# The last step of a running sum taken into the TensorE product that reads it, and a division moved behind the second layer

## The chip, the cores and the metric

The kernel runs on one core of one Trainium2 chip. The metric is the device time of one execution in microseconds (us), median of several runs. The engines of the core are named as in the profile: PE (TensorE, matrix products into PSUM), DVE (VectorE), ACT (ScalarE), POOL (GpSimd) and SP, which here only issues transfers. Transfers run on the core's 16 DMA engines.

## The reference

Two stages. First an attention read between tokens `x` (8 batches, 8 heads, 512 tokens, 64 wide) and a state of 32 rows: each token reads the state (`xread`) and each state row reads the tokens (`sread`). Both results together, 4352 rows of 512, are the input of a mixture of experts with soft slots:

```python
logits = x @ phi                          # 4352 x 32 slots
d = exp(logits - logits.max(0)); d /= d.sum(0) + 1e-9
slot_input = (d.T @ x).reshape(E, 4, D)   # 8 experts, 4 slots each
for e in range(E):
    h = np.maximum(slot_input[e] @ w1[e], 0.0)   # w1: 8 x 512 x 1024
    slot_out[e] = h @ w2[e]                      # w2: 8 x 1024 x 512
c = softmax(logits, axis=1)
out = c @ slot_out
```

All data is fp32. The weights w1 and w2 are 16.8 MB each, `x` is 8.4 MB, and the output is 4352 rows of 2 KB.

## The kernel before

The attention stage goes batch by batch. Its steps are short functions, and the string `ORDER` writes down in which order they are issued (`T.3` is step `T` of group 3). Every engine runs its own instructions in that order. Batches go in pairs, four groups in all; each group gives a part of the logits and, without a second pass over the tokens, a part of `slot_input`.

The sum over tokens runs as a streaming softmax. `nm_all` holds the running maximum, `al_all` the factor by which the old sums shrink when the maximum grows, `l_row` the running sum of exponentials and `y` the running sum of weighted inputs, kept in 128 partitions as (4 parts of 32 slots) x 128. A group's step is: `T` (PE) makes `t_ps`, the attention weights multiplied into the exponentials; `tt` (DVE) turns its 32 x 32 blocks out of PSUM; `Px` (PE) multiplies by the state into `px_ps`; `Y` (DVE) does `y = y * al + px_ps`. The state rows add two steps of their own (`Ps`, `Ys`).

After the last group, `Wd` multiplies `l_row` by a matrix of ones and zeros (`rep`) into `l_ps` to add the 4 parts, `We` (DVE, two instructions, L633 and L634) adds 1e-9 and takes the reciprocal `rl`, `Yf` (ACT, L638) makes a diagonal matrix `rd` of `rl`, and `SI` (PE, L642) is one product of `y` and `rd`: it transposes `y` and divides by l together. `SIe` copies the four blocks of its result to `si_m` by four DVE copies. `si_m` is the stationary operand of the first layer (L697, `h_ps`). The steps `W.256` and `W.128` are products of the identity whose results nobody reads.

Then both layers run for all experts with the weights as moving operand: the first layer in two halves (`h_ps`), a turn and the ReLU, the second layer (`so_ps`, L760), and `so_sum`, which adds 4 row blocks by `rep` (`sum_ps`) and copies the result to `so_r` by ACT (L788). From `so_r` and the softmax `c` come the output tiles (`o`), copied by ACT and DVE and sent by SP (L809, L811, L834, L852).

Buffers: the small PSUM results share one tag `ms` with three buffers, taken in turn (`mtile`). A new tile waits until all readers of the tile three before it are done. The weights stream from HBM the whole time through SP into the pools `big` and `pairs`; a weight transfer is issued when its buffer is free. The pool `const` lies ahead of them in SBUF; each of its tiles is rounded up to 32 bytes a partition, and with its sizes as they are the pool `big` starts at a multiple of 512 bytes.

Of the kernel before, what the change touches and what calls it, by code (L numbers as in the profile page):

```python
# [8 lines left out]
F32 = mybir.dt.float32  # L9
# [6 lines left out]
P = 128  # L16
B = 8
S = 512
NS = 32
D = 64  # L20
# [30 lines left out]
mul.7.1 R.6.0 x1.6.0 R.6.1 mk.2 bm.2 U.1 l1.6.0 ae.5.1 nme.2 mul.7.0 rr.6 srT.7 ae.4.0 sr.6 mul.6.0 dx.2 A.4.1 aT.7.0  # L51
srT.6 aT.6.0 srTe.7 dT.2 srTe.6 Px.1 dTe.2 mul.6.1 Ls.1 V.1 Lse.1 Ue.1 Y.1 Lr.1 ae.4.1 Lx.6.0 aT.6.1 al.2 Lx.6.1
Lx.7.0 T.2 aT.7.1 msx.1 Lx.7.1 Ve.1 tt.2 dsx.1 A.6.1 pv.3 Lu.1 als.1 mx.3 mkd.3 ae.6.1 A.7.1 bm.3 nme.3 keep.3 Lu.2
Lus.1 A.7.0 lkp.1 A.6.0 dx.3 D.1 dT.3 ad.7.1 Px.2 ad.6.0 ae.7.0 dTe.3 Ps.1 al.3 Y.2 Ys.1 Lu.3 T.3 tt.3 Wd We Px.3
W.256 Yf Y.3 SI W.128 SIe
"""
SR_BUFS = 1
AN = 2
# [5 lines left out]
def attention_soft_moe(ctx: ExitStack, tc: tile.TileContext, x0, x1, x, st0, st1, w1, w2a, w2b, out_x, out_s):  # L64
# [7 lines left out]
    pe, act, dve, pool = nc.tensor, nc.scalar, nc.vector, nc.gpsimd  # L72

    cp = ctx.enter_context(tc.tile_pool(name="const", bufs=1))
# [9 lines left out]
    for b in range(B):  # L84
        t = big.tile([P, 4, NJ, 2 * D], F32, tag="big", name=f"x{b}")
        if b == 0:
            for i in range(4):
                v = x0[i].rearrange("p (g j c) -> p g j c", g=1, j=NJ)
# [58 lines left out]
    ident = cp.tile([P, P], F32, name="ident")  # L147
# [16 lines left out]
    G_sb = cp.tile([P, B, 2, NS], F32, name="G_sb")  # L164
# [5 lines left out]
    al_all = cp.tile([P, B + 2], F32, name="al_all")  # L170
    l_row = cp.tile([P, 1], F32, name="l_row")
    y = cp.tile([P, P], F32, name="y")

    with ExitStack() as actx:
        wk = actx.enter_context(tc.tile_pool(name="work", bufs=1))
        sm = actx.enter_context(tc.tile_pool(name="small", bufs=2))
# [4 lines left out]
        Q = [dict() for _ in range(2)]  # L181
        X2 = [dict(b=g) for g in GROUPS]
# [5 lines left out]
        Z = {"n": 0}  # L188

        def half(name):  # L190
            return wk.tile([P, S], F32, tag="h", name=name, bufs=NH)

        def mtile(shape, name):
            return ps_m.tile(shape, F32, tag="ms", name=name)
# [119 lines left out]
        def copy_of(eng):  # L314
            return act.copy if eng is act else dve.tensor_copy
# [313 lines left out]
            pe.matmul(Z["lp"], rep, l_row, start=True, stop=True)  # L629

        def We():
            Z["rl"] = sm.tile([P, 1], F32, tag="rl", name="rl", bufs=1)
            dve.tensor_scalar_add(Z["rl"], Z["lp"], EPS)  # L633
            dve.reciprocal(Z["rl"], Z["rl"])  # L634

        def Yf():
            Z["rd"] = sm.tile([P, P], F32, tag="ds", name="rd", bufs=1)
            act.mul(Z["rd"], ident, Z["rl"])  # L638

        def SI():  # L640
            Z["p"] = mtile([P, 4, NS], "si_ps")
            pe.matmul(Z["p"].rearrange("p k n -> p (k n)"), y, Z["rd"], start=True, stop=True)  # L642

        def warm(n):
            p = ps_t.tile([P, S], F32, tag="tr", name=f"warm{n}_ps")
# [4 lines left out]
        def slots(t, k):  # L650
            lead = 32 if k else 0
            v = t[:, 256 * k - lead : 256 * k - lead + 288]
            return v.rearrange("p (e c) -> p e c", c=36)[:, :, lead : lead + 4]

        si_m = []

        def windows():
            for k in range(2):
                si_m.append(half(f"si_m{k}"))
                pool.memset(si_m[k], 0.0)  # L660

        def SIe():
            for k in range(4):
                dve.tensor_copy(slots(si_m[k // 2], k % 2), Z["p"][:, k, :].rearrange("p (e c) -> p e c", c=4))

        steps = dict(
            G=G, Ge=Ge, X=X, xe=xe, S=Sc, q=q, m1=m1, sub=sub, x1=x1, l1=l1, rr=rr, mul=mul, aT=aT, m2=m2, e2=e2,
            E=E_, ee=ee, A=A_, ae=ae, R=R_, sr=sr, srT=srT, srTe=srTe, Lx=Lx, keep=keep, mx=mx, mk=mk,
            pv=pv, bm=bm, nme=nme, al=al, dx=dx, Lu=Lu, dT=dT, dTe=dTe, T=T_, tt=tt, U=U, Ue=Ue, Px=Px, Y=Y,
            Ls=Ls, Lse=Lse, Lr=Lr, msx=msx, als=als, dsx=dsx, Lus=Lus, lkp=lkp, D=Dn, V=V, Ve=Ve, Ps=Ps, Ys=Ys,  # L670
            xd=xd, ed=ed, ad=ad, srTd=srTd, Wd=Wd, We=We, Yf=Yf, SI=SI, SIe=SIe, windows=windows, mkd=mkd, W=warm, keepd=keepd, dTd=dTd, Ud=Ud, Vd=Vd,
        )
        load_w(NBIG - B + 2 * NPAIR)
        order = ORDER.split()
# [55 lines left out]
        c = [half(f"c{i}") for i in range(3)]  # L730
        c = [v[:, 0 : t.shape[1]].rearrange("p (t n) -> p t n", n=NS) for v, t in zip(c, c_t)]
# [22 lines left out]
        so, so_sb, so_r = {}, {}, {}  # L754
# [26 lines left out]
        def so_sum(k, half_of=0):  # L781
            c = slice(P * half_of, P * half_of + P)
            p = mtile([P, P], f"sum_ps{k}_{half_of}")
            pe.matmul(p, rep, so_sb[k][:, c], start=True, stop=True)
            i = k + half_of
            if i % 2 == 0:
                so_r[i // 2] = half(f"so_r{i // 2}")[:, 0:256]
            act.copy(so_r[i // 2][:, P * (i % 2) : P * (i % 2) + P], p)  # L788

        def out(k, q):  # L790
            hf, col = k // 2, 128 * (k % 2)
# [96 lines left out]
        so_copy(0)  # L888
        more(1)
        so_sum(0)  # L890
        more(1)
        so_sum(0, 1)
        out(0, 0)
        more(5)
# [4 lines left out]
        so_copy(2)  # L899
        out(1, 1)  # L900
        so_sum(2)
        more(4)
        out_st(0)
# [46 lines left out]
```

## Time and profile before

| | |
|---|---|
| median of 3 runs | 129.68 us (129.62 to 129.85) |
| the profiled execution: its time, and its span from first to last instruction | 129.54 us, 127.8 us |
| busy share of the span: PE, DVE, ACT, POOL | 91%, 68%, 60%, 35% |
| bytes moved, mean rate over the span | 51.74 MB, 405 GB/s |
| granted clock of PE | 1.00 until 121 us, then 0.50; mean 0.974 |

The span is what the trace's times count in; 1.74 us of the execution lie around it. Times in the rows below are us from the span's start.

### The profile page before, as it was taken

What the parts mean: (1) busy time and instruction counts of PE and PEld (TensorE: products, weight loads), DVE (VectorE), ACT (ScalarE), POOL (GpSimd) and SP (SyncE); (2) the same over time, 40 slices, a digit from 0 to 9 for tenths busy, and PEclk for the clock granted to TensorE, in tenths of its full rate; (3) what the DMA queues carried; (4) which work ended last, traced back from release to release, by engine and by line L of the source; (5) the groups of instructions that cost most, each with busy time, mean ns of one, the idle gap of its engine ahead of it and who ended that gap; (6) DMA issues with size and microseconds to landing.
All of it is one profiled execution on the core that took longest, in us unless ns stands there. A gap on an engine that the chain in (4) does not pass through costs nothing.

```text
span 127.8 us, 4698 instructions
## 1 busy us (share of the span) xinstructions
PE 116.7 (91%) x1992; PEld 80.5 (63%) x1992; DVE 86.7 (68%) x194; ACT 76.9 (60%) x189; POOL 44.8 (35%) x63
## 2 busy tenths in 40 slices
PE   5989999999999999999999999999999999998600
PEld 2737686789686869858767869952465655575200
DVE  2348999999999999999986759019930355442700
ACT  4039999999999999999965711310100445635700
POOL 3005266391947467557882105803500000000000
PEclk9999999999999999999999999999999999999955
DMA  4999999999999999999999999999999999999993
GB/s 130 345 410 423 423 426 423 428 423 421 423 423 426 416 436 416 421 431 418 426 418 433 416 421 398 448 423 441 413 441 415 436 383 412 421 419 420 386 430 139
DMA packets 8229, 51.74 MB, mean 405 GB/s; under 512 B 912, under 2 KB 1040, under 8 KB 3216
## 3 DMA queue, kind: packets, MB, share of 16 engines
q1 hardware_dynamic: 7920, 50.92, 95.9%
q10 hardware_dynamic: 288, 0.52, 1.1%
q8 instruction: 15, 0.25, 0.7%
q14 instruction: 6, 0.05, 0.1%
HBM read 42.53 MB, written 8.91 MB: 403 GB/s over the span
## 4 chain that ended last, share of the span: by engine, by line
PE 72%; DVE 10%; DMA 6%; ACT 3%; issue 2%; SPq 1%; POOL 0%; DVEq 0%; ACTq 0%; POOLq 0%
PE so_ps L760 12%; PE h_ps L697 11%; PE xt_ps L226 8%; PE o L796 7%; DMA st_phi<-st_in 6%; PE sc L245 5%; PE sr_ps L343 4%; PE an_ps L309 4%; PE eT_ps L309 4%; PE lt L378 3%; PE t_ps L503 2%; DVE sums L274 2%; DVE q L258 2%; DVE aT L290 1%; DVE m L263 1%
## 5 line engine op out<-in xcount | busy, mean ns | idle before, releaser
L267 POOL TENSOR_TENSOR q<-q,m 128x512 f32<-128x512 f32 x16 | 16.8, 1051 | 15.7 <-DVE m L263 5.2
L231 ACT ACTIVATE xt<-xt_ps 128x512 f32<-128x512 f32 x30 | 18.0, 618 | 5.7 <-PE xt_ps L226 5.5
L226 PE MATMUL xt_ps<-ident,x 128*128 128x128 f32 x128 | 18.4, 282 | 0.5 <-DMA x<-x_in 0.5
L285 POOL TENSOR_TENSOR q<-q,rr 128x512 f32<-128x512 f32 x16 | 16.6, 1051 | 5.1 <-DVE rr L280 3.6
L226 PEld LDWEIGHTS xt_ps<-ident,x 128*128 128x128 f32 x128 | 14.6, 144 | 3.8 <-PE sc L245 1.4
L760 PE MATMUL so_ps<-w,h_m 128*32 128x128 f32 (+1 forms) x376 | 15.5, 309 | 0.0
L807 DVE COPY out<-o 128x512 f32<-128x512 f32 x14 | 9.2, 687 | 9.0 <-PE o L796 8.8
L760 PEld LDWEIGHTS so_ps<-w,h_m 128*32 128x32 f32 x376 | 10.4, 110 | 7.2 <-issue 4.6
L697 PE MATMUL h_ps<-w,si_m 128*32 128x512 f32 x128 | 14.4, 594 | 0.1
L296 DVE TENSOR_REDUCE nm<-sc 128x1 f32<-128x512 f32 x16 | 10.6, 670 | 2.2 <-PE sc L245 2.2
L806 ACT COPY out<-o 128x512 f32<-128x512 f32 x14 | 7.7, 588 | 6.8 <-PE o L796 6.7
L697 PEld LDWEIGHTS h_ps<-w,si_m 128*32 128x32 f32 x128 | 9.1, 110 | 3.9 <-issue 2.9
L301 ACT ACTIVATE e<-sc,nm 128x512 f32<-128x512 f32 x16 | 11.3, 709 | 0.4 <-DVE nm L296 0.2
L258 DVE STREAM_TRANSPOSE q<-sc 128x512 f32<-128x512 f32 x16 | 11.1, 695 | 0.1
L290 DVE STREAM_TRANSPOSE aT<-q 128x512 f32<-128x512 f32 x16 | 10.9, 689 | 0.3 <-POOL q L285 0.2
L343 PE MATMUL sr_ps<-x,eT 128*32 128x64 f32 x512 | 10.5, 221 | 0.1
L274 DVE TENSOR_REDUCE sums<-q 128x16 f32<-128x512 f32 x16 | 10.4, 663 | 0.2 <-ACT q L270 0.2
L263 DVE TENSOR_REDUCE m<-q 128x16 f32<-128x512 f32 x16 | 10.4, 658 | 0.0
L270 ACT ACTIVATE q<-q 128x512 f32<-128x512 f32 x16 | 10.4, 650 | 0.0
L309 PE MATMUL eT_ps<-ident,e 128*128 128x128 f32 x64 | 9.8, 279 | 0.0
L245 PE MATMUL sc<-xt,st_phi 64*32 64x512 f32 x128 | 9.6, 601 | 0.0
L343 PEld LDWEIGHTS sr_ps<-x,eT 128*32 128x32 f32 x512 | 8.7, 110 | 1.5 <-issue 1.0
(126 smaller groups left out, 186.2 us busy)
## 6 DMA issues: line engine op xcount, KB each, us to landing
w<-w_in SPq DMA_DIRECT2D x16, 1024.0 KB, 19.7
w<-w2b_in SPq DMA_DIRECT2D x4, 2048.0 KB, 15.0
x<-x_in SPq DMA_DIRECT2D x7, 1024.0 KB, 13.9
w<-w2a_in SPq DMA_DIRECT2D x6, 1024.0 KB, 19.5
out_x<-out SPq DMA_DIRECT2D x6, 1024.0 KB, 5.8
out_x<-out SPq DMA_DIRECT2D x4, 512.0 KB, 4.7
w<-w2a_in SPq DMA_DIRECT2D x4, 256.0 KB, 14.5
x<-x_in ACTq DMA_DIRECT2D x2, 256.0 KB, 3.9
```

The source lines that it names most:

```text
L226: pe.transpose(p[:, P * j : P * j + P], xb[b][:, g, j, :], ident)
L231: act.mul(r[f"xt{g}"], r[f"xp{g}"], 0.125)
L245: pe.matmul(r[f"sp{h}"][32 * g : 32 * g + 32, :], st_t(b, g)[64 * h : 64 * h + 64, :], r[f"xt{g}"][64 * h : 64 * h + 64, :], start=True, s ...
L258: dve.transpose(r[f"q{h}"], r[f"sp{h}"])
L267: pool.tensor_tensor(v, v, R[b][f"m1{h}"].broadcast_to([P, 16, NS]), op=ALU.subtract)
L274: dve.tensor_reduce(out=v, in_=R[b][f"qv{h}"], axis=AX.X, op=ALU.add)
L285: pool.tensor_tensor(v, v, r.broadcast_to([P, 16, NS]), op=ALU.mult)
L290: dve.transpose(r[f"aT{h}"], r[f"q{h}"])
L309: pe.transpose(p[:, j, :], r[f"{src}{h}"][:, P * j : P * j + P], ident)
L343: pe.matmul(r["srp"][32 * g : 32 * g + 32, h, :], r[f"eT{h}"][:, j, 32 * g : 32 * g + 32], xb[b][:, g, j, D * h : D * h + D], start=(j == ...
L697: pe.matmul(h_ps[hf][32 * kt : 32 * kt + 32, :], si_m[kt // 2][:, 256 * (kt % 2) + 32 * e : 256 * (kt % 2) + 32 * e + 32], w1t[hf, e, kt], ...
L760: pe.matmul(so[k][32 * i : 32 * i + 32, :], h_m[hf][:, 256 * i + 32 * e : 256 * i + 32 * e + 32], w(i), start=(hf == 0 and e == 0), stop=( ...
```

## The change

The last group's step of `y` is no longer done by DVE. `Yf` now makes a diagonal of the last group's factor `al` in place of `rl`. `SIa` multiplies `y` by it (4 products into two PSUM tiles, left open), and `SIb` adds to the same tiles the state times the last group's turned `t_ps` (4 products). For that `ttz` writes the turned blocks into a zeroed tile `tz`, the upper 64 partitions to one place and the lower 64 to another (two DVE transposes). `tz` reuses half of `G_sb`, zeroed on POOL in the step `windows`. `Px.3`, `Y.3`, `tt.3` and the two `W` steps are gone. `Wd` and `We` stand between `SIa` and `SIb`; `rl` is now used in `so_sum`, where ACT multiplies by it in place of copying, and it lives in the pool `const`. Two of the four copies of `SIe` move to ACT.

```diff
-Lus.1 A.7.0 lkp.1 A.6.0 dx.3 D.1 dT.3 ad.7.1 Px.2 ad.6.0 ae.7.0 dTe.3 Ps.1 al.3 Y.2 Ys.1 Lu.3 T.3 tt.3 Wd We Px.3
-W.256 Yf Y.3 SI W.128 SIe
+Lus.1 A.7.0 lkp.1 A.6.0 dx.3 D.1 dT.3 ad.7.1 Px.2 ad.6.0 ae.7.0 dTe.3 Ps.1 al.3 Y.2 Yf Ys.1 Lu.3 T.3 ttz SIa Wd We SIb
+SIe
...
         def We():
-            Z["rl"] = sm.tile([P, 1], F32, tag="rl", name="rl", bufs=1)
+            Z["rl"] = cp.tile([P, 1], F32, name="rl")
...
         def Yf():
             Z["rd"] = sm.tile([P, P], F32, tag="ds", name="rd", bufs=1)
-            act.mul(Z["rd"], ident, Z["rl"])
-
-        def SI():
-            Z["p"] = mtile([P, 4, NS], "si_ps")
-            pe.matmul(Z["p"].rearrange("p k n -> p (k n)"), y, Z["rd"], start=True, stop=True)
+            act.mul(Z["rd"], ident, al_all[:, X2[-1]["c"]])
+
+        def ttz():
+            for gh in range(2):
+                rows = slice(64 * gh, 64 * gh + 64)
+                dve.transpose(
+                    tz[rows, gh].rearrange("p g h n -> p (g h n)"),
+                    X2[-1]["tp"][rows].rearrange("p g h n -> p (g h n)"),
+                )
+
+        def SIa():
+            Z["p"] = [mtile([P, 2, NS], f"si_ps{g2}") for g2 in range(2)]
+            rd = Z["rd"].rearrange("p (a g n) -> p a g n", a=2, g=2)
+            for g2 in range(2):
+                for h in range(2):
+                    pe.matmul(
+                        Z["p"][g2][64 * h : 64 * h + 64],
+                        y[:, D * h : D * h + D],
+                        rd[:, :, g2, :],
+                        start=True,
+                        stop=False,
+                    )
+
+        def SIb():
+            for g2 in range(2):
+                for h in range(2):
+                    pe.matmul(
+                        Z["p"][g2][64 * h : 64 * h + 64],
+                        Q[1]["st"][:, 2 + g2, D * h : D * h + D],
+                        tz[:, :, g2, h, :],
+                        start=False,
+                        stop=True,
+                    )
...
+        tz = G_sb[:, 0:4].rearrange("p b g n -> p (b g n)").rearrange("p (a g h n) -> p a g h n", a=2, g=2, h=2)
+
         def windows():
+            pool.memset(tz, 0.0)
...
         def SIe():
             for k in range(4):
-                dve.tensor_copy(slots(si_m[k // 2], k % 2), Z["p"][:, k, :].rearrange("p (e c) -> p e c", c=4))
+                v = Z["p"][k % 2][:, k // 2, :].rearrange("p (e c) -> p e c", c=4)
+                copy_of(act if k % 2 else dve)(slots(si_m[k // 2], k % 2), v)
...
-            act.copy(so_r[i // 2][:, P * (i % 2) : P * (i % 2) + P], p)
+            act.mul(so_r[i // 2][:, P * (i % 2) : P * (i % 2) + P], p, Z["rl"])
```

## Rows read from the trace of the kernel before

**Rows 1.** The page, DMA queues: packets, MB, share of 16 engines' span

```profile
q1 hardware_dynamic: 7920, 50.92, 95.9%
...
q8 instruction: 15, 0.25, 0.7%
```

**Rows 2.** Chain that ended last: start, length, what

```profile
73.81 0.33 DVE tt L514
...
74.18 0.45 PE px_ps L540 x16
...
75.77 0.20 DVE si_m L664
...
76.01 9.06 PE h_ps L697 x80
...
116.72 0.28 ACT so_r L788
```

**Rows 3.** Timeline of SP: start and length of three issues

```profile
85.10 0.42 SPq L114 DMA_DIRECT2D w<-w2b_in  x1
...
102.17 0.35 SPq L809 DMA_DIRECT2D out_x<-out  x1
...
121.24 0.35 SPq L811 DMA_DIRECT2D out_x<-out  x1
```

**Rows 4.** Those three issues, in the same order: KB, us to landing

```profile
w<-w2b_in SPq DMA_DIRECT2D x1, 2048.0 KB, 20.7
...
out_x<-out SPq DMA_DIRECT2D x1, 512.0 KB, 5.0
...
out_x<-out SPq DMA_DIRECT2D x1, 1024.0 KB, 5.6
```

**Rows 5.** All output transfers, grouped: count, KB each, median us to landing

```profile
out_x<-out SPq DMA_DIRECT2D x6, 1024.0 KB, 5.8
out_x<-out SPq DMA_DIRECT2D x4, 512.0 KB, 4.7
...
out_s<-out_s SPq DMA_DIRECT2D x2, 256.0 KB, 5.1
```

**Rows 6.** Stretches: us, busy of PE, PEld, DVE, ACT, POOL; PEclk, DMA share, GB/s

```profile
20.00:30.00 10.00, 10.00 (x214) 7.96 (x208) 9.67 (x19) 9.69 (x22) 5.47 (x6) 1.00 1.01 423
...
64.00:66.00 2.00, 1.69 (x32) 1.13 (x31) 1.66 (x4) 1.14 (x5) 1.74 (x3) 1.00 1.04 434
...
119.00:119.50 0.50, 0.50 (x6) 0.21 (x4) 0.23 (x1) 0.30 (x1) 0.00 (x0) 1.00 0.56 238
...
121.00:121.50 0.50, 0.00 (x0) 0.00 (x0) 0.18 (x1) 0.03 (x1) 0.00 (x0) 0.67 1.00 410
...
125.00:125.50 0.50, 0.00 (x0) 0.00 (x0) 0.00 (x0) 0.00 (x0) 0.00 (x0) 0.50 0.55 229
...
126.00:126.50 0.50, 0.00 (x0) 0.00 (x0) 0.00 (x0) 0.00 (x0) 0.00 (x0) 0.50 0.24 98
```

**Rows 7.** Timeline of `Wd` and `We`: start, length, engine, line

```profile
73.64 0.38 PE L629 MATMUL l_ps<-l_row,rep 128*128 128x1 f32 x2
...
74.06 0.16 DVE L633 TENSOR_SCALAR rl<-l_ps 128x1 f32<-128x1 f32 x1
...
74.25 0.16 DVE L634 RECIPROCAL rl<-rl 128x1 f32<-128x1 f32 x1
```

**Rows 8.** Groups by shape, 60 to 78 us: busy us, mean ns | idle before

```profile
L514 DVE STREAM_TRANSPOSE tt<-t_ps 128x128 f32<-128x128 f32 x2 | 0.6, 316 | 1.4 <-PE t_ps L503 1.4
...
L638 ACT ACTIVATE rd<-ident,rl 128x128 f32<-128x128 f32 x1 | 0.4, 402 | 1.7 <-DVE rl L634 1.7
```

**Rows 9.** The tile `so_r`: its writers, ns min/median/max

```profile
L788 ACT COPY so_r<-sum_ps x4: 266/266/284, 99.5 to 116.7; 128x128 f32<-128x128 f32 x4
```

**Rows 10.** Timeline of POOL around the step `windows`: start, length

```profile
58.67 0.99 POOL L660 MEMSET si_m<- 128x512 f32 x2
...
62.21 1.05 POOL L285 TENSOR_TENSOR q<-q,rr 128x512 f32<-128x512 f32 x1 [0.40 <-ACT mk L413]
```

More of the change, by code (lines that the diff above doesn't have):

```diff
@@ L670, in attention_soft_moe @@
             Ls=Ls, Lse=Lse, Lr=Lr, msx=msx, als=als, dsx=dsx, Lus=Lus, lkp=lkp, D=Dn, V=V, Ve=Ve, Ps=Ps, Ys=Ys,
-            xd=xd, ed=ed, ad=ad, srTd=srTd, Wd=Wd, We=We, Yf=Yf, SI=SI, SIe=SIe, windows=windows, mkd=mkd, W=warm, keepd=keepd, dTd=dTd, Ud=Ud, Vd=Vd,
+            xd=xd, ed=ed, ad=ad, srTd=srTd, Wd=Wd, We=We, Yf=Yf, ttz=ttz, SIa=SIa, SIb=SIb, SIe=SIe, windows=windows, mkd=mkd, W=warm, keepd=keepd, dTd=dTd, Ud=Ud, Vd=Vd,
         )
```

## The prediction

> **What bounds the kernel now.** I read the chain of waits first, because the change shortens a stretch of it. From the end of the last `T` the chain runs over one DVE transpose, `Px`, the identity product, `SI`, and a DVE copy into the first layer [rows 2]: DVE starts at 73.81 us and `h_ps` at 76.01, so this passage takes 2.20 us. From there the chain is PE, almost without a gap, to the last output tile. Read alone, this view says that PE's order sets the end and that a shorter passage shortens the kernel by as much.
>
> Then I read the transfers, because the chain is followed from the last instruction and does not ask whether a transfer that was issued in time could have run any sooner. The queue of loads and stores alone keeps 16 DMA engines busy for 95.9% of the span [rows 1]. To see whether the rest is a wait for the compute I compare landings, each an issue time plus its time to landing. The last weight transfer is issued at 85.10 and lands at 85.10 + 20.7 = 105.8: it stood some 15 us in the queue, since 2 MB need 5 us at the rate of the stretches. The first output piece lands at 102.17 + 5.0 = 107.2, that is 1.4 us after it, and 0.52 MB at 423 GB/s need 1.24 us [rows 3, 4, 6]. The last output lands at 121.24 + 5.6 = 126.8. Between these two outputs 8704 - 512 = 8192 KB [rows 5], 8.39 MB, land in 19.6 to 19.7 us: 426 to 428 GB/s, no slower than the loads' 423 in mid-kernel [rows 6]. A transfer counts as landed when its last share is in, so these landings are those of whichever DMA engine is furthest behind. That engine has no free time between 85 us and the end. It carries a fixed number of bytes, and nothing that PE does after 74 us takes bytes from it.
>
> The Trainium skill (DMA: Bandwidth & Descriptors, Why a DMA increments its semaphore by 16 and not by 1) says that the engines of a transfer finish independently and that the full count means that all have landed. The stretches agree with that: the DMA share is 0.55 in 125.0 to 125.5, and 0.24 is still left in 126.0 to 126.5 [rows 6].
>
> The engines are not equal. At 119.0 to 119.5 the share is 0.56 for half a microsecond: about half of them have run dry and wait for the next output, while the others are never out of work [rows 6]. At the end about half stop around 125.3 and the rest a microsecond later. The slack of the compute is therefore about 1 us, which is the lead of the early half over the late one. What puts one engine behind shows in part in the page: 15 fetches of instructions, 0.25 MB [rows 1]. They are 0.7% of 16 engines' time, 0.007 x 16 x 127.8 / 15 = 0.95 us each, an estimate, if each falls on one engine.
>
> **The change part by part.**
>
> *Removed from the passage:* `tt.3`, `Px.3`, `Y.3`, `W.256`, `SI`, `W.128`, in all 2.20 us from 73.81 to 76.01 [rows 2].
>
> *`ttz`:* two transposes of 64 partitions with the 128 columns that `tt` has. A transpose of 128 x 128 takes 316 ns [rows 8]. No row shows one of 64 partitions. If only columns count, two take 0.63 one after the other; if half the rows were half the price, 0.32 together. I take 0.60, since the two may overlap a little. End 74.41.
>
> *`Wd`:* its tile `l_ps` is the third from the `ms` tag after `t_ps`, `si_ps0` and `si_ps1`; with three buffers taken in turn it falls on `t_ps` and must wait until `ttz` has read it. Before, it ran beside `tt` for nothing. Now it starts at about 74.45 (0.04 from the transpose's end to the product behind it, 74.14 to 74.18 [rows 2]) and takes 0.38 to 74.83 [rows 7]. Behind it in PE's order stands `SIb`, which needs `ttz` anyway.
>
> *`We`:* 74.06 to 74.41 before, 0.35 [rows 7], after `Wd` and one hand-over: 74.87 to 75.22. It stands ahead of `SIe` in DVE's order, so DVE is not free before.
>
> *`SIa` and `SIb`:* four products of 64 columns each. `SIa` has all it needs before `ttz` ends and is hidden by it; uncovered it would cost what `SIb` does. `SIb`: the nearest row is `px_ps`, 8 products issued as 16 in 0.45 [rows 2]; with half as many of twice the width I take the same, between 0.25 and 0.60. It starts 0.1 to 0.38 after 74.45 behind `Wd`, and ends about 75.15, beside `We`.
>
> *`SIe`:* DVE copies at 75.22 and `h_ps` follows 0.24 later, as 75.77 to 76.01 before [rows 2]: 75.46. The copies that ACT takes run beside those of DVE; ACT is idle here.
>
> Sum of the passage: 76.01 - 75.46 = 0.55 us earlier. Worst bound (`SIb` of 0.60 wholly behind `Wd`, then copies): 75.71, so 0.30. Best bound (`ttz` in 0.32): 75.18, so 0.83.
>
> *`so_r`:* ACT multiplies by a column instead of copying. The copy takes 266 ns [rows 9]; the one row with a column as factor, `rd`, also 128 x 128, takes 402 [rows 8]. Four times 0.14, from 0 to 0.14 each. Three are covered by PE's products of `so_ps`; the last stands on the chain at 116.72 [rows 2]. Cost 0.13.
>
> *POOL's memset of `tz`:* half the width of those of `si_m`, which take 0.99 for two [rows 10], so 0.25 to 0.5. POOL then waits 0.40 before 62.21 [rows 10], which covers most of it; uncovered, at most 0.1 reaches ACT, and PE's work until 73.8 hides that. `Yf` moves to a stretch in which ACT waits.
>
> So PE's chain, and with it every output's issue, comes 0.55 - 0.13 = 0.42 us earlier (0.16 to 0.83). What is late next is the transfers: the late DMA engines take each output 0.42 us later after its issue than now. No byte and no transfer is removed, and the weights' issues wait for buffers with some 10 us of queue ahead of them. At the end this is worth 0, at most 0.1, as the 1.4 us from the last weights to the first output hold 0.1 to 0.2 more than its bytes need. The sum against the profiled execution: 129.54 - 0 to 0.1; that execution is 0.14 below the median, so against the median of 129.68 I say 129.65.
>
> **The rivals.**
>
> *The chain sets the end.* All of the 0.42 us would arrive: 129.26. For it speaks that the chain of waits is unbroken, and that half of the DMA engines do run dry at 119.2. Against it: the other half does not, and the run ends with the other half. Chance 0.08.
>
> *The kernel gets slower because buffers move.* `rl` is a new tile in the pool `const`, 32 bytes, and every pool behind it, weights and outputs included, then starts 32 bytes past its old multiple of 512. If each 8 KB row of a transfer then pays for the 32 bytes that stick out, it takes 1/256 longer: 0.4% of the some 123 us in which the queue is busy [rows 1], +0.5 us: 130.2. It decides as soon as the price is above 0.2% of the transfers' time, for they have no slack. The Trainium skill (DMA: Bandwidth & Descriptors, How a descriptor splits into AXI transactions) says that a piece must start at a 256-byte boundary and that one which does not pays for the bytes before it, with a beat of 32 bytes; by that rule it is +0.5 as well. No row of this kernel compares the two starts at this offset. Chance 0.06.
>
> *PE's clock falls.* The two identity products go, and PE waits some 0.3 us before `Wd` and 0.3 before `h_ps`. The granted clock stayed at 1.00 through 64 to 66 us, where PE was idle for 0.31 us, and fell to 0.50 in 121.0 to 121.5, with PE out of work for good [rows 6]. So a wait of this size did not lower it, but two come close together here. At half speed 80 products of the first layer take 9 us more than their 9.06 [rows 2]; with 1.4 us of slack (1.0 and the 0.42 gained) it shows in the time only when the lower level lasts over 2.8 us, and at the full 9 us it gives 129.7 + 7.6 = 137.3. The Trainium skill (TensorE: Matmul & The Clock Gate, What's actually happening) says that activity releases the clock's throttle, which speaks against taking products out; the fall at 121 us agrees. Chance 0.03.
>
> **How the numbers follow.** The forecast, no gain because the late DMA engines set the end, has 0.83; its own range is 129.5 to 129.8. Under 0.2%, 0.26 us, can't be told from no change here; the three runs before differ by 0.23. Faster by over 0.2%: the first rival, and 0.01 of the forecast, 0.09. Slower: the second and third, 0.09. Same: 0.82. The range for 8 in 10 is the forecast's, widened to 129.35 and 130.0 for a partial gain or a smaller price of the shift; the rivals' own times lie outside it.
>
> **What would show it.** Right: `h_ps` starts near 75.5, the last `so_r` takes 0.4, the last output is issued near 120.8, and yet lands near 126.8, its time to landing up from 5.6 to 6.0; the dip of the DMA share at 119 moves or fills, and the span stays 127.8. Wrong in the first way: the last landing moves with its issue. In the second: landings of 1 MB further apart, mean rate below 405 GB/s by 0.4% or more, at unchanged issue times. In the third: a granted clock below 1.00 between 75 and 90 us. If `Wd` starts before `ttz` ends, the buffers don't go as I say.

## The result, and the profile after

The changed kernel takes 131.12 us (130.88 to 131.36, six runs) against 129.89 (129.62 to 130.25, six runs) of the kernel before, run beside it: ratio 1.0093 [1.0075, 1.0111]. It is slower by 1.2 us; I had said 129.65 and no change. The profiled execution takes 131.11 us with a span of 129.3; before it was 129.54 and 127.8.

I read the transfers first. The page of the changed kernel, its totals and two of its DMA issues (count, KB each, median us to landing):

```profile
DMA packets 8229, 51.74 MB, mean 400 GB/s; under 512 B 912, under 2 KB 1040, under 8 KB 3216
...
out_x<-out SPq DMA_DIRECT2D x6, 1024.0 KB, 7.3
out_x<-out SPq DMA_DIRECT2D x4, 512.0 KB, 6.1
```

The same 51.74 MB go at 400 GB/s instead of 405, and in the median an output takes 1.4 to 1.5 us longer from issue to landing [rows 5]. The stretches say where the rate is lost, first the changed kernel, then three of the kernel before (columns as in [rows 6]):

```profile
20.00:30.00 10.00, 10.00 (x206) 7.72 (x194) 9.68 (x19) 9.68 (x22) 5.70 (x6) 1.00 1.02 417
30.00:40.00 10.00, 9.88 (x221) 7.93 (x217) 9.93 (x24) 9.87 (x26) 5.30 (x7) 1.00 1.01 415
40.00:50.00 10.00, 10.00 (x214) 7.64 (x199) 9.93 (x22) 9.72 (x27) 6.92 (x7) 1.00 1.01 415
...
110.00:115.00 5.00, 5.00 (x96) 2.83 (x96) 1.99 (x3) 2.47 (x6) 0.00 (x0) 1.00 1.02 425
```

```profile
30.00:40.00 10.00, 9.87 (x217) 7.68 (x207) 9.93 (x23) 9.88 (x26) 5.54 (x7) 1.00 1.01 424
40.00:50.00 10.00, 10.00 (x213) 7.94 (x202) 9.93 (x23) 9.78 (x27) 6.93 (x7) 1.00 1.01 424
...
110.00:115.00 5.00, 5.00 (x98) 2.86 (x98) 2.13 (x4) 2.61 (x6) 0.00 (x0) 1.00 1.01 420
```

Already between 20 and 50 us, long before any instruction that the diff edits, the loads run at 417, 415 and 415 GB/s, against 423 [rows 6], 424 and 424 before. The DMA engines are as busy as then (1.01 to 1.02); each byte takes longer. From 110 to 115 us, where only outputs move, nothing is lost: 425, where the same stretch of before moved 420.

The issues of SP (start and length), and after them the time to landing of the last two weight transfers and of the last output:

```profile
84.64 0.90 SPq L114 DMA_DIRECT2D w<-w2b_in  x2
102.31 0.94 SPq L841 DMA_DIRECT2D out_x<-out  x2
...
121.79 1.13 SPq L843 DMA_DIRECT2D out_x<-out  x1
```

```profile
w<-w2b_in SPq DMA_DIRECT2D x2, 2048.0 KB, 20.2
...
out_x<-out SPq DMA_DIRECT2D x1, 1024.0 KB, 6.6
```

The last two weight transfers of the kernel before:

```profile
84.63 0.90 SPq L114 DMA_DIRECT2D w<-w2b_in  x2
```

```profile
w<-w2b_in SPq DMA_DIRECT2D x2, 2048.0 KB, 18.6
```

These two are issued at the same time in both kernels, and take 20.2 us in the median of the two, where they took 18.6: they land 1.6 us late. The first output, 6.5 us to landing, lands at 102.31 + 6.5 = 108.8, which is 1.6 after the 107.2 of before. The last lands at 121.79 + 6.6 = 128.4, 1.6 after 126.8. So the whole loss is there when the loads end, and the outputs add nothing to it: 19.6 us from the first landing to the last, as before.

The passage from the last `T` to the first layer (start, length, engine):

```profile
73.28 1.06 PE L503 MATMUL t_ps<-an,dT 128*32 128x128 f32 x32
73.37 0.40 ACT L638 ACTIVATE rd<-ident,al_all 128x128 f32<-128x128 f32 x1
...
74.26 0.61 PE L653 MATMUL si_ps<-rd,y 128*64 128x64 f32 x8
74.42 0.64 DVE L643 STREAM_TRANSPOSE G_sb<-t_ps 64x128 f32<-64x128 f32 x2 [0.41 <-PE t_ps L503]
...
75.21 0.35 PE L629 MATMUL l_ps<-l_row,rep 128*128 128x1 f32 x2 [0.34 <-DVE G_sb L643]
...
75.50 0.45 PE L664 MATMUL si_ps<-G_sb,sv 128*64 128x64 f32 x8
75.61 0.16 DVE L633 TENSOR_SCALAR rl<-l_ps 128x1 f32<-128x1 f32 x1 [0.54 <-PE l_ps L629]
75.80 0.16 DVE L634 RECIPROCAL rl<-rl 128x1 f32<-128x1 f32 x1
75.88 0.29 DVE L696 COPY si_m<-si_ps 128x32 f32<-128x32 f32 x2
76.00 0.27 ACT L696 COPY si_m<-si_ps 128x32 f32<-128x32 f32 x2 [2.23 <-PE si_ps L664]
...
76.13 0.73 PE L729 MATMUL h_ps<-w,si_m 128*32 128x512 f32 x3 [0.18 <-DVE si_m L696]
```

The last `T` of the kernel before:

```profile
72.66 1.06 PE L503 MATMUL t_ps<-an,dT 128*32 128x128 f32 x32
```

From the start of `T` to `h_ps` it is 76.13 - 73.28 = 2.85 us. Before, `T` started at 72.66 and `h_ps` at 76.01 [rows 2], 3.35. The passage gained 0.50, and `T`, late by 0.62, took it away again.

### The profile page after: what moved, and what is told of

It reads as the page before. It is cut to its first block, busy times and chain, and to the rows that moved or that the text cites. A ratio compares the mean times of both kernels' runs of the same rounds, so it can differ in the third digit from the quotient of the medians.

```text
span 129.3 us, 4686 instructions
## 1 busy us (share of the span) xinstructions
PE 116.1 (90%) x1986; PEld 78.4 (61%) x1986; DVE 86.6 (67%) x192; ACT 77.6 (60%) x191; POOL 44.9 (35%) x64
## 2 busy tenths in 40 slices
DMA packets 8229, 51.74 MB, mean 400 GB/s; under 512 B 912, under 2 KB 1040, under 8 KB 3216
## 4 chain that ended last, share of the span: by engine, by line
PE 69%; DVE 14%; DMA 6%; issue 2%; SPq 1%; ACT 1%; POOL 0%; DVEq 0%; ACTq 0%; POOLq 0%
PE so_ps L792 12%; PE h_ps L729 11%; PE xt_ps L226 8%; PE o L828 7%; DMA st_phi<-st_in 6%; PE sc L245 5%; PE an_ps L309 4%; PE eT_ps L309 4%; PE sr_ps L343 4%; PE lt L378 2%; DVE sums L274 2%; DVE q L258 2%; PE t_ps L503 2%; DVE nm L296 2%; DVE aT L290 2%
## 5 line engine op out<-in xcount | busy, mean ns | idle before, releaser
L729 PEld LDWEIGHTS h_ps<-w,si_m 128*32 128x32 f32 x128 | 7.3, 110 | 5.7 <-issue 3.2
## 6 DMA issues: line engine op xcount, KB each, us to landing
w<-w2a_in SPq DMA_DIRECT2D x6, 1024.0 KB, 20.2
```

Source lines behind the costliest of these rows:

```text
L729: pe.matmul(h_ps[hf][32 * kt : 32 * kt + 32, :], si_m[kt // 2][:, 256 * (kt % 2) + 32 * e : 256 * (kt % 2) + 32 * e + 32], w1t[hf, e, kt], ...
```

## The experiments

My theory: `rl` in the pool `const` moves all load buffers off their alignment, and this alone is the loss; the steps of the change neither cost nor gain, since transfers hide the gain. The first rival: something in the changed steps costs the time. The second: the shift is the cause, but it is the engines that read shifted tiles that pay for it, and not the loads. "Before" is in each case the kernel before, run on the same chip.

**The change without the shift.** `rl` goes back into the pool `small`, where it was; all else is the changed kernel.

```diff
-            Z["rl"] = cp.tile([P, 1], F32, name="rl")
+            Z["rl"] = sm.tile([P, 1], F32, tag="rl", name="rl", bufs=1)
```

> The changed kernel with one line undone: rl is again a tile of the small pool, so every buffer that transfers write or read starts at a multiple of 512 bytes as before; all steps of the change stay. Theory (the 32-byte shift of the buffers costs the 1.2 us): 1 MB loads land 2.44 us apart again, not 2.49, and the time is within 0.3 us of the kernel before, about 129.8. Rival (the new steps cost it: the memset of tz, ACT's share of SIe, the multiplication by rl): the time stays near 131.1 and loads stay 2.49 apart.

Measured: 129.66 us (12 runs) against 129.71, ratio 0.9996 [0.9977, 1.0014]. Its PE timeline, the stretch of the dip, SP's last issue and that issue's time to landing:

```profile
72.74 1.06 PE L503 MATMUL t_ps<-an,dT 128*32 128x128 f32 x32
...
75.59 3.82 PE L729 MATMUL h_ps<-w,si_m 128*32 128x512 f32 x32 [0.18 <-DVE si_m L696]
```

```profile
119.00:119.50 0.50, 0.50 (x6) 0.17 (x4) 0.24 (x1) 0.29 (x1) 0.00 (x0) 1.00 1.07 434
```

```profile
120.82 0.44 SPq L843 DMA_DIRECT2D out_x<-out  x1
```

```profile
out_x<-out SPq DMA_DIRECT2D x1, 1024.0 KB, 6.1
```

The passage is again 2.85 us, the last output is issued 0.42 us before 121.24, and lands at 126.9, as before. The loss is gone and no gain has come in its place: the first rival falls, and what remains of the change is worth nothing that shows (the interval leaves room for a gain of 0.3 us).

**The shift without the change.** An unused tile of 32, 64 or 128 bytes stands in the pool `const` of the kernel before (32 shown).

```diff
+    pad = cp.tile([P, 8], F32, name="pad")
+    pool.memset(pad, 0.0)
```

> The kernel before with an unused 32-byte tile added to the pool const, zeroed once on POOL; no step changed. Theory (shift): +1.2 to +1.6 us, about 131.2, loads of 1 MB 2.49 apart from the first one on, outputs still 2.44 apart. Rival (new steps): 129.9, as before.

> The kernel before with an unused 64-byte tile in const: buffers start 64 bytes past a multiple of 512. If any start off a multiple of 256 costs (the boundary that the Trainium skill names), +0.5 to +1.6 us, 130.4 to 131.4. If a multiple of 64 is enough, 129.9.

> The kernel before with an unused 128-byte tile in const. With a boundary of 256: +0.5 to +1.6 us, as for 64. If a multiple of 64 or 128 is enough: 129.9. The load into st_phi, which starts 128 bytes past a multiple of 256 in the kernel before and lands no later than its neighbours, speaks for 129.9.

Measured, against 129.71: 131.19, ratio 1.0112 [1.0077, 1.0146], with 32 bytes; 131.06, 1.0093 [1.0061, 1.0126], with 64; 130.99, 1.0090 [1.0056, 1.0123], with 128. An unused tile costs as much as the whole change did. A price in proportion to the bytes that stick out is ruled out: four times the offset does not cost more. For 128 bytes I had leant to 129.9, because the load into `st_phi` starts at such an offset already and lands no later than its neighbours. That was no test: it is one load of 0.5 MB, and a few ns more for each of its 128 rows can't be seen in its landing.

**Another multiple.** Tiles of 256 bytes go from `const` to `small`, so that the load buffers start at a multiple of 256 that is not one of 512.

```diff
-    nm_all = cp.tile([P, B + 2], F32, name="nm_all")
...
-    l_row = cp.tile([P, 1], F32, name="l_row")
...
+        nm_all = sm.tile([P, B + 2], F32, tag="nm", name="nm_all", bufs=1)
+        l_row = sm.tile([P, 1], F32, tag="lr", name="l_row", bufs=1)
...
-        mc = [cp.tile([P, v.shape[1], 1], F32, name=f"mc{i}") for i, v in enumerate(c)]
+        mc = [sm.tile([P, v.shape[1], 1], F32, tag=f"mc{i}", name=f"mc{i}", bufs=1) for i, v in enumerate(c)]
```

> The kernel before with 256 bytes of its constants (running maximum, running sum, row maxima of c) allocated in the pool small, so that all buffers of transfers start at a multiple of 256 that is no multiple of 512; no step changed. If the boundary that counts is 256 bytes: 129.7, loads of 1 MB 2.44 to 2.45 apart. If it is 512: about 131, loads 2.49 apart. A rival that blames the mere moving of buffers expects about 131 too.

Measured: 129.69 against 129.73, 0.9989 [0.9964, 1.0013]. A shift by 256 bytes is free.

**The shift of the working tiles alone.** The unused 32 bytes stand behind the pools `big` and `pairs`, so that only the tiles behind these are moved, and few of the loads with them.

```diff
+    gap = ctx.enter_context(tc.tile_pool(name="gap", bufs=1))
+    pad = gap.tile([P, 8], F32, name="pad")
+    pool.memset(pad, 0.0)
```

> The kernel before with a 32-byte gap behind the pool pairs: only the work tiles of ACT, DVE, POOL and PE and the last five small loads are shifted, big and pairs are not. If the loads' start costs: at most 0.2 us more, 129.7 to 129.9, since only 1.5 MB of loads are shifted. If the engines' own accesses to shifted tiles cost: about 131.

Measured: 129.85 against 129.73, 1.0003 [0.9989, 1.0016]. Engines that work on shifted tiles lose nothing that shows, and zeroing the unused tile on POOL costs nothing that shows either. The weights that PE reads out of the load buffers stay in place in this run; for these the trace of the changed kernel answers, where a product of `h_ps` takes 594 ns in the mean, as in the kernel before. So the second rival falls. Two stretches each of the kernels with 32 bytes ahead of everything, with 128, with 256, and with 32 behind the load buffers, in this order:

```profile
20.00:30.00 10.00, 10.00 (x217) 7.91 (x205) 9.68 (x19) 9.67 (x22) 5.51 (x6) 1.00 1.02 417
...
40.00:50.00 10.00, 10.00 (x214) 7.60 (x199) 9.73 (x21) 9.78 (x27) 6.62 (x7) 1.00 1.01 416
```

```profile
20.00:30.00 10.00, 10.00 (x210) 7.75 (x198) 9.68 (x19) 9.69 (x22) 5.67 (x6) 1.00 1.02 421
...
40.00:50.00 10.00, 10.00 (x215) 7.63 (x200) 9.84 (x22) 9.78 (x27) 6.83 (x7) 1.00 1.01 416
```

```profile
20.00:30.00 10.00, 10.00 (x210) 7.82 (x198) 9.68 (x19) 9.69 (x22) 5.61 (x6) 1.00 1.01 424
...
40.00:50.00 10.00, 10.00 (x209) 7.94 (x202) 9.93 (x22) 9.82 (x27) 7.01 (x7) 1.00 1.01 422
```

```profile
20.00:30.00 10.00, 10.00 (x214) 7.88 (x202) 9.68 (x19) 9.69 (x22) 5.55 (x6) 1.00 1.01 424
...
40.00:50.00 10.00, 10.00 (x216) 7.82 (x201) 9.89 (x22) 9.78 (x27) 6.88 (x7) 1.00 1.01 423
```

The last column divides the four, though single stretches come close to each other (421 with 128 bytes, 422 with 256). Over the whole of 20 to 50 us they run at 416, 419, 423 and 424 GB/s, in this order, and the kernel before at 423.

The traces also hold the time of every DMA packet, and a packet here is one row of a transfer. Mean ns of a packet, worked out from these:

| kernel | 3712 rows of 8 KB, loads | 512 rows of 16 KB, loads | 768 rows of 8 KB, outputs |
|---|---|---|---|
| before | 312.4 | 613.9 | 311.0 |
| 256 bytes | 311.7 | 613.9 | 311.1 |
| the change, `rl` in `small` | 312.2 | 612.8 | 312.1 |
| the change | 317.0 | 619.0 | 312.7 |
| 32 bytes | 317.7 | 619.1 | 312.2 |
| 128 bytes | 314.8 | 617.7 | 313.3 |

The rows of the loads themselves take longer where the buffers are shifted. With 32 bytes a row of 16 KB loses about as much as one of 8 KB: 5.1 and 5.2 ns, against 4.6 and 5.3. The kernel with 64 bytes is not in the table, as its traced execution took 132.49 us, 1.4 above its median.

**Is the gain of the passage real?** If transfers hide it, it must appear when there are fewer of them. Once the loads of the first layer's second half for the experts 6 and 7 (2 MB), once the last 2 MB load of the second layer is left out; other weights are used in their place. Each is done to the kernel before and to the change with `rl` in `small`. The second edit:

```diff
+            if (layer, k, e) == (3, 1, 4):
+                for i in range(32):
+                    w2t[3, k, e + i // 8, i % 8] = w2t[3, k, i // 8, i % 8]
+                continue
```

> The kernel before without the loads of the second half of w1 for experts 6 and 7 (2 MB; expert 5's is used in their place, so the output is not the reference's). If transfers set the end: up to 4.9 us of it go, but only until PE's chain sets the end; from its last issues, unqueued, I expect the span to end about 1.4 us earlier, 128.2. If PE's chain set the end already: 129.7, no change.

> The changed kernel with rl in the small pool and the same two loads left out. If the change's gain is real but hidden by the transfers, it shows here: 0.4 us below the kernel before without those loads, about 127.8. If the change gains nothing: the same as that kernel.

> The kernel before without the last load (2 MB of w2, the one issued at 85.10; another expert's weights are used in its place, so the output is not the reference's). The queue is the same until then. If the late DMA engine's bytes set the end, the time falls, but only until the outputs, 21 us of transfers from the first issue at 102.2 on, set it: about 0.5 us, 129.2. If PE's chain sets the end at the last output: 129.7, no change.

> The changed kernel with rl in the small pool and the same last load left out. Now the first output's issue is what the end hangs on, and the passage saved should show: 0.4 us below the kernel before without that load, 128.8. If the change gains nothing on PE's chain: equal to it.

Without the earlier 2 MB: before's form 129.33 against 129.73, 0.9962 [0.9939, 0.9984]; the change's form 129.10, 0.9938 [0.9914, 0.9961]. Both miss what was expected, and their intervals overlap: inconclusive. The first profile shows why so little came of 2 MB, 5 us of transfers:

```profile
74.00:76.00 2.00, 1.92 (x26) 1.27 (x24) 1.00 (x7) 0.40 (x1) 0.00 (x0) 1.00 0.73 267
76.00:78.00 2.00, 2.00 (x22) 1.86 (x21) 1.93 (x4) 0.00 (x0) 0.67 (x1) 1.00 0.64 221
78.00:80.00 2.00, 2.00 (x25) 1.86 (x20) 1.36 (x3) 0.81 (x2) 1.65 (x3) 1.00 0.80 170
```

The queue runs dry here: the next loads are issued at 77.90, 2.23 us after `h_ps` starts (75.67), just as in the kernel before (78.24 and 76.01), since they wait for buffers that the first layer frees. Part of the saved time lies there, and I take it that this part does not reach the end.

Without the last load: before's form 129.29 against 129.83, 0.9958 [0.9938, 0.9977]; the change's form 128.66, 0.9913 [0.9894, 0.9931]. The second pair of intervals does not overlap, and the difference is 0.63 us. The last issue of each (first before's form) and the time to landing:

```profile
121.24 0.61 SPq L815 DMA_DIRECT2D out_x<-out  x1
```

```profile
out_x<-out SPq DMA_DIRECT2D x1, 1024.0 KB, 5.4
```

```profile
120.59 0.54 SPq L847 DMA_DIRECT2D out_x<-out  x1
```

```profile
out_x<-out SPq DMA_DIRECT2D x1, 1024.0 KB, 5.3
```

The stretch in which the first outputs are issued, before's form:

```profile
100.00:105.00 5.00, 5.00 (x102) 2.96 (x105) 2.58 (x4) 2.42 (x5) 0.00 (x0) 1.00 0.42 168
```

The loads have ended before the outputs begin. With no loads queued in front of them, an issue that comes 0.65 earlier lands 0.75 earlier: 125.9 against 126.6. Of the 0.65 the passage gives 0.50; the rest was there before it, as `T` starts at 72.50 and 72.65. In the full kernel an issue 0.42 earlier landed no earlier at all. This shows that the gain is real and that the queue of loads hides it.

**How much slack has the compute?** One or four more identity products stand in the passage of the kernel before.

```diff
-W.256 Yf Y.3 SI W.128 SIe
+W.256 W.512 Yf Y.3 SI W.128 SIe
```

> The kernel before with one more identity product of 512 columns (0.86 us of PE) in the passage behind T.3, and nothing else. If the transfers set the end with about 1 us of slack for the compute: 129.7 to 129.9. If PE's chain sets it: +0.86, 130.6.

> The same with four such products (3.44 us of PE). If the transfers set the end and the slack is 0.8 to 1.4: +2.0 to +2.6, 131.8 to 132.4. If PE's chain sets it: +3.4, 133.2. If the compute never mattered: 129.8.

With one: 130.27 against 129.83, 1.0039 [1.0012, 1.0067]. With four: 133.67, 1.0297 [1.0275, 1.0320]. Both miss what was expected: the first lies between its two values, the second above all three. The kernel with one, its PE timeline:

```profile
72.80 1.06 PE L503 MATMUL t_ps<-an,dT 128*32 128x128 f32 x32
...
76.76 2.76 PE L697 MATMUL h_ps<-w,si_m 128*32 128x512 f32 x21
```

Its passage is 3.96 us, 0.61 longer than the 3.35 of before, and 0.44 of that arrives (0.16 to 0.87 by the interval). So less than about 0.45 us of slack stood behind the compute, and not the 1 us I had read. The kernel with four, SP's issue of the 2 MB loads and two stretches after it:

```profile
81.57 2.04 SPq L114 DMA_DIRECT2D w<-w2b_in  x2
```

```profile
82.00:83.00 1.00, 1.00 (x15) 0.95 (x11) 0.96 (x3) 0.63 (x1) 0.65 (x2) 1.00 1.21 276
83.00:84.00 1.00, 1.00 (x15) 0.95 (x11) 0.07 (x1) 0.51 (x1) 1.00 (x3) 1.00 0.54 147
```

These loads are issued 3.33 us after the 78.24 of before, and the queue runs low: 276 and 147 GB/s where the same two stretches of before moved 502 and 455. The first output is issued 3.33 later too (105.50) and the last 3.34 (124.58). That accounts for 3.3 of the 3.84 us. The last output also lands later behind its issue, 6.3 us for 5.6, and why it does is open.

## Why the prediction was wrong, step by step

**The step that failed** is the price of the rival "the kernel gets slower because buffers move". The mechanism stood there with its place (`rl` in `const`), its threshold (above 0.2% of the transfers' time) and its sign in the profile (mean rate below 405, every load slower), and all three held. I sized it by bytes: 32 of 8192, 0.4%, +0.5 us, and gave it 0.06. By that size a row of 8 KB would take 1.2 ns more. Measured, it takes 4.6 more in the changed kernel, and a row of 16 KB 5.1 more. So the price goes by the row and not by the byte, and one row costs about four times what I took. With the rows spread evenly over 16 engines it is (3712 x 4.6 + 512 x 5.1) / 16 = 1.2 us, an estimate, and 1.2 us is what the medians lose. The two profiled executions lie further apart, 131.11 and 129.54, and their last weights land 1.6 us apart; the 0.4 beyond the rows' own time is not explained. Nor is the kernel with 128 bytes: its rows lose 2.4 and 3.8 ns, 0.7 us by the same sum, and it lost 1.28.

The Trainium skill (DMA: Bandwidth & Descriptors, How a descriptor splits into AXI transactions) puts the boundary at 256 bytes. The trace agrees: 32, 64 and 128 cost 1.3 to 1.5 us, 256 costs nothing. It counts the price in beats of 32 bytes before the start, by which 128 bytes would cost four times as much as 32 (an estimate worked out from the page's beats). The measurement differs: 1.28 us against 1.48, with overlapping intervals, and with 32 a row of 8 KB lost 1.5 to 1.7% where one beat in 256, the same estimate, is 0.4%. The page also speaks of what a transaction reads. Here the loads, which write the shifted buffers, pay, while the median row of the outputs, which read them, takes 309 ns in the kernel before and in the changed one alike.

**The chance** was worse than the price. "No row of this kernel compares the two starts" was true, and an unmeasured price that touches every row of the resource that I had just called the bound deserved a wide bound above: I kept the one size by bytes and left all others out of the range. My own sentence says that the transfers have no slack, so each 0.1% of a load was 0.1 us of the end.

**What bounds the kernel:** right for a compute that comes earlier. The pair without the last load shows that the gain of the passage arrives when the loads are out of the way, and the change without the shift shows no gain when they are not. For a compute that comes later it was wrong. The slack was mis-sized: "about 1 us" came from the lead of the early DMA engines over the late ones, and the kernel with one more product puts it under 0.45. The two limits lie close together: with the last load gone, the time is 129.29, only 0.54 below the 129.83 with it. "Some 10 us of queue ahead of them" was wrong as well: in the kernel with four products a delay of 3.3 us already leaves the queue short at 83 us, since the loads issued there wait for buffers that PE frees.

**The passage:** 0.55 predicted, 0.50 measured, inside 0.30 to 0.83. The two transposes took 0.64 (0.60 taken), so half the partitions cost the full price. `Wd` waited for them as said, since its buffer was that of `t_ps`; the hand-over behind the second transpose was 0.15 and not 0.04. `SIb` took the 0.45 of its nearest row. `SIa` and `Yf` were hidden.

**`so_r`:** four rows of 367 to 385 ns against 266 to 284 [rows 9], 0.10 each; I took 0.13. The changed kernel's writers of that tile:

```profile
L820 ACT ACTIVATE so_r<-sum_ps,rl x4: 367/368/385, 99.7 to 116.9; 128x128 f32<-128x128 f32 x4
```

**The issues:** 0.42 us earlier predicted; without the shift the last went from 121.24 to 120.82, exactly that. The match is in part luck. The passage gave 0.50 and `so_r` took 0.10, but `T` came 0.08 late, and the first 80 products of the first layer took 0.1 less, which I had not forecast. The chain of the changed kernel shows it too, against 9.06 in [rows 2]:

```profile
76.13 8.96 PE h_ps L729 x80
```

The likely reason is that ACT now copies half of `si_m` beside DVE; no run isolates it. The last output without the shift landed 6.1 after instead of 5.6, at 126.9, with the dip at 119 filled (1.07 for 0.56). All of "what would show it: right" is found there. The sign of the second rival is found in the changed kernel, with the last weights issued when they were before; other issues moved, the last output's by 0.55.

**The clock:** 1.00 in every stretch from 20 to 120 us; this rival did not happen.

## What to carry to other kernels

Where transfers set the end, look first at what a change does to the addresses of their buffers: here a 32-byte tile in the first pool cost 1.2 us, more than the 0.4 to 0.6 that the edit gains at best. Place small late tiles behind the load buffers, or keep what lies ahead of these at a multiple of 256 bytes, and price an unknown cost by the unit that can pay it (row, packet, byte), with the dearest of them as the upper bound. A passage that becomes shorter pays only as far as the other limit allows; take that distance from an experiment that delays it, since the lead of one DMA engine over another is not slack.

## What the runs showed of the hardware

- A load into a buffer that starts 32 bytes past a multiple of 256 loses about 5 ns a row, for rows of 8 KB and of 16 KB alike: 416 GB/s for 423. With 128 bytes past it the rows lose 2.4 and 3.8 ns (419 GB/s), and the kernel about as much as with 32. I had expected a price that grows with the offset.
- Stores out of the same shifted buffers lose nothing that shows: a row of 8 KB takes 309 ns in the median before, with 32 bytes and with 128; from 110 to 115 us they run at 425 GB/s in the changed kernel against 420 before, and it is 19.6 us from the first output's landing to the last's in both.
- A DVE transpose of 64 partitions takes as long as one of 128: two in 0.64 us, against 0.316 for one [rows 8].
